# A three-stage chain (attention, gated feed-forward, mixture attention) on one core: a written table of the order of all operations, other PSUM banks, and filler products

## The chip, the cores and the metric

One Trainium2 chip, one of its cores. The time is microseconds (us) of device time of one execution. The kernel before was timed three times: 550.66, 550.70 and 551.35 us, median 550.7. Beside that one execution was profiled.

## The reference, cut to what matters

Four batches go through three stages, all in float32. Shapes: batch 4, 12 heads, 448 positions, head size 64, model size 768, inner size 1024, 4 experts.

```python
# 1: attention with a soft cap
scores = cap * tanh((q @ k.T) / 8 / cap)
attn = exp(scores - max) / (sum + 1e-9)
x = heads_side_by_side(attn @ v)              # [448, 768]
# 2: gated feed-forward with a convolution along the positions
h = maximum(x @ w_in, 0)                      # [448, 1024]
gate = 1 / (1 + exp(-conv3(h, conv_w)))
x = (h * gate) @ w_out                        # [448, 768]
# 3: four causal attention experts, the two best by x @ w_gate weighted
for e in range(4):
    y_e = softmax(causal((x @ wq[e]) @ (x @ wk[e]).T / 8)) @ (x @ wv[e]) @ wo[e]
out = sum(w_e * y_e)
```

## The kernel before, in words

Precision comes from splitting: a float32 value is written as a high part h that TensorE multiplies in its fast float32r form and a rest l, and a product is h·h + h·l + l·h, three TensorE products where one would do. Only the value products, the sums and the filler products run as plain float32; the profile counts each of these twice, since each is two passes.

Names of the stages, as used below. A *pair* is two heads that share 128 rows; a batch has six, numbered g = 0 to 23 over all batches. `qk` (line 560) makes the scores of a pair in four blocks of keys (three of 128, one of 64 that both heads share): products into PSUM, then ScalarE takes the hyperbolic tangent out of PSUM (896 columns for a block of two heads, 448 for the shared one) and the exponential (1792 and 1344 columns). `pv` (line 608) multiplies by the values. For g under `JOINT` it uses eight products per pair, each 128 rows by 64 columns of the array, and the shared block has rows of zeros for the other head. From `JOINT` on an even pair has six products and the odd one after it ten, of which four are 64 by 64, and two banks stay open, 7 and 2. `sums` and `recip` (lines 646, 662) give the sums of the exponentials and one over them, `x_unit` (line 744) spreads these over the head's rows by two products of 64 rows per unit, three units a batch: VectorE multiplies the attention output by them out of PSUM, ScalarE and VectorE split it into h and l. `f_unit` (line 755) multiplies by `w_in` in two half sums of nine products, `conv_gate` (line 778) makes convolution and gate in four ScalarE and four VectorE operations of 448 columns. For the first `EARLY_N[b]` of the eight row blocks of a batch that happens right behind `f_unit`; for the others `prep_g` (line 891) loads the raw h back from DRAM and does it later. `wi_prep` (line 730) decodes and splits `w_in` during batch 0: per piece one ScalarE absolute value of 256 columns and VectorE work. `fold_mm` folds `w_out` and the projection weights into one matrix between stage 2 and stage 3, after which per batch `v_unit`, `proj_unit`, `scores2`, `norm2`, `tr2`, `pv2` and `wo_unit` (lines 979 to 1163) do stage 3.

PSUM has eight banks of 512 columns. `qk` writes pairs of banks in turn, 3 and 4 and then 5 and 6. `pv` of batch 0 writes bank 1 for pairs 0, 2 and 4 and bank 7 for the others. `x_unit` takes banks 2, 0, 1 in a ring, `pv2` bank 7.

What sets the order. No engine's instructions are written in the order in which they run. Each call (`pl.mm`, `pl.act`, `pl.tt`, `pl.load` and so on) records an operation with its cost and the operations that it depends on (`Plan.add`, line 127). At the end `Plan.issue` (line 210) runs a list scheduler (`Plan.schedule`, line 154) several times, with costs, a wish for a place (`at`, shifted by the table `BIAS`) and windows, takes the order that ends first by its own reckoning, and issues every operation in that order. Each engine then works its own queue strictly in that order, and waits at an instruction until what that instruction needs is done. All DMAs stand in one queue, SP's.

So in the profile nearly all products have the line of a helper (305), all ScalarE operations 245, all VectorE operations 253, transposes 309, DMAs 314.

At the very start eight products of zeros (`WARM`) run on TensorE into bank 7 before the first data have landed.

Of the kernel before, what the change touches and what calls it, by code (L numbers as in the profile page):

```python
# [14 lines left out]
NP = H // 2  # L15
# [23 lines left out]
JOINT = 10  # L39
# [7 lines left out]
WARM = 8  # L47
ABS_DVE = (0, 0, 0, 0)
PV_1 = (0, 2, 4)
# [20 lines left out]
EARLY_N = (1, 7, 7, 0)  # L70
# [3 lines left out]
WINDOW = 0  # L74
STAY = 2000.0
ROUNDS = 5
# [14 lines left out]
class Plan:  # L91

    PAGE = 256


    DRAIN = 97.0
    OPEN = {(128, 128): 107.0, (64, 128): 107.0, (128, 64): 53.0, (64, 64): 53.0, (128, 32): 13.0}  # L100
    RATE = 320.0
    HOP = {"pe": 200.0, "act": 190.0, "dve": 170.0, "pool": 150.0, "dma": 1500.0}

    def __init__(self, nc):
        self.nc, self.ops, self.pos, self.seen, self.bias, self.kind = nc, [], 0.0, {}, 0.0, None

    def pages(self, ap):
# [19 lines left out]
    def add(self, eng, cost, calls, outs, ins, keys_out=(), keys_in=(), size=0, modes=None):  # L127
        op = Op()
        op.modes, op.kind = modes, self.kind
        op.eng, op.cost, op.calls, op.pos, op.n, op.size = eng, cost, calls, self.pos, len(self.ops), size  # L130
        op.after, op.bias = [], self.bias
        before = {}
        touched = [(k, w, False) for a in ins for k, w in self.pages(a)] + [(k, True, False) for k in keys_in]
        touched += [(k, w, True) for a in outs for k, w in self.pages(a)] + [(k, True, True) for k in keys_out]
        for key, whole, write in touched:
            past = self.seen.setdefault(key, [])
            for o, w in past:
                if (write or w) and o is not op:
                    before[o.n] = o
            if write and whole:  # L140
                past[:] = [(op, True)]
            elif (op, write) not in past:
                past.append((op, write))
        for o in before.values():
            o.after.append(op)
        self.ops.append(op)
        return op

    def latency(self, a, b):
        if a.eng == b.eng and a.eng != "dma":  # L150
            return 0.0 if a.eng == "pe" else 130.0
        return self.HOP[a.eng] + a.size / self.RATE

    def schedule(self, place, links, window, back=False):

        ops, todo = self.ops, [0] * len(self.ops)
        for l in links:
            for n, _ in l:
                todo[n] += 1
        ready, start, end = ([0.0] * len(ops) for _ in range(3))  # L160
        free, open_, pick, order = {}, {}, {}, []
        for e in self.HOP:
            free[e], open_[e] = 0.0, [o.n for o in ops if o.eng == e and not todo[o.n]]
        wire, cold, changed, mode, lands = 0.0, COLD_0, set(self.HOP), None, []
        if not back:
            free["dma"] = 800.0
        while len(order) < len(ops):
            for e in changed:
                if open_[e]:
                    t = max(free[e], min(ready[n] for n in open_[e])) + (window if e in ("pe", "act", "dve") else 0.0)  # L170
                    if e == "pe" and not back:
                        n = min((place[n] + (ops[n].modes[0] != mode) * STAY, n) for n in open_[e] if ready[n] <= t)[1]
                    else:
                        n = min((place[n], n) for n in open_[e] if ready[n] <= t)[1]
                    pick[e] = max(free[e], ready[n]), e, n
                    if e == "dma" and len(lands) >= 8:

                        pick[e] = max(pick[e][0], lands[-8]), e, n
                else:
                    pick.pop(e, None)  # L180
            t, e, n = min(pick.values())
            cost, more = ops[n].cost, 0.0
            if e == "pe" and not back:

                if t - free[e] > 2500.0:
                    cold = max(cold, t + 3600.0)
                if t < cold:
                    cost += min(cost, (cold - t) / 2)
                if ops[n].modes[0] != mode:
                    cost += self.DRAIN + self.OPEN[ops[n].modes[0]]  # L190
                mode = ops[n].modes[1]
# [1116 lines left out]
```

## Time and profile before

| | |
|---|---|
| median of three runs | 550.7 us |
| profiled execution, span of its instructions | 549.1 us |
| between the two (what lies around the span, and the spread of runs) | 1.6 us |
| TensorE products, busy | 539.9 us, 98% |
| VectorE, busy | 447.7 us, 82% |
| ScalarE, busy | 395.3 us, 72% |
| batch 0 of stage 1 | about 5 to 58 us |
| batches 1 to 3 of stage 1, with stage 2 of the batch before | to about 264 us |
| rest of stage 2, folding of the weights | to about 347 us |
| stage 3 of the four batches | to the end |

In the profile a product's end is modelled, so "busy" is no measure of how much faster TensorE could be; the distance from one start to the next is. "Idle before" names the engine that ended the wait. A row "x16" merges sixteen instructions of one form that follow each other.

### The profile page before, as it was taken

How to read it: one execution, taken by the hardware profiler on the slowest of the kernel's cores; microseconds unless marked ns; L12 is line 12 of the kernel's file. 1: busy time of each engine (PE TensorE's matmuls, PEld its weight loads, DVE VectorE, ACT ScalarE, POOL GpSimd, SP SyncE). 2: the span in 40 equal slices, each digit the busy share in tenths (PEclk: the TensorE clock that was granted, in tenths of full speed). 3: DMA queues.
4: the chain of work that ended last, by engine and by line, in shares of the span. 5: the costliest groups of instructions: out<-in, count | busy, mean ns of one | idle time of the engine just before them, and what ended most of it. 6: DMA issues, size and time to landing. Idle time of an engine off the chain costs nothing.

```text
span 549.1 us, 9130 instructions
## 1 busy us (share of the span) xinstructions
PE 539.9 (98%) x3170; PEld 420.1 (77%) x3170; DVE 447.7 (82%) x980; ACT 395.3 (72%) x736; POOL 24.5 (4%) x100
## 2 busy tenths in 40 slices
PE   7999999999999999999999999999999999999997
PEld 5444596556785567656799999989988997999886
DVE  6989999968788799878978999846867988946763
ACT  6999967898789997995645678625754977624751
POOL 8600000000000000000000000100000000000000
PEclk9999999999999999999999999999999999999999
DMA  7655425342224320224385632326433314413414
GB/s 257 194 184 171 152 91 162 110 124 87 65 86 122 109 84 32 77 83 121 111 240 164 219 115 73 108 70 149 112 91 104 97 53 123 126 45 87 105 57 145
DMA packets 38942, 64.61 MB, mean 118 GB/s; under 512 B 6896, under 2 KB 27632, under 8 KB 38896
## 3 DMA queue, kind: packets, MB, share of 16 engines
q1 hardware_dynamic: 38896, 64.02, 39.6%
q8 instruction: 25, 0.41, 0.3%
q14 instruction: 21, 0.17, 0.1%
HBM read 41.72 MB, written 12.85 MB: 99 GB/s over the span
## 4 chain that ended last, share of the span: by engine, by line
PE 78%; DVE 9%; ACT 8%; issue 2%; DMA 2%; SPq 0%; DVEq 0%; ACTq 0%
PE ps L305 76%; ACT fm L245 7%; DVE fm L253 6%; DVE rm L253 3%; PE ps L309 2%; ACT rm L245 1%; DMA fm<-w_in 1%; DMA fm<-g_dram 1%; SPq L314 0%; DVE ps L253 0%; DVEq L253 0%; ACTq L245 0%
## 5 line engine op out<-in xcount | busy, mean ns | idle before, releaser
L305 PE MATMUL ps<-rm 128*128 128x448 f32 (+4 forms) x2382 | 423.7, 355 | 4.8 <-ACT fm L245 3.7
L305 PEld LDWEIGHTS ps<-rm 128*128 128x128 f32 (+1 forms) x2382 | 367.8, 188 | 66.4 <-ACT fm L245 21.5
L245 ACT ACTIVATE fm<-fm 128x448 f32<-128x448 f32 (+8 forms) x247 | 178.0, 747 | 31.6 <-DVE fm L253 15.9
L253 DVE SCALAR_TENSOR_TENSOR fm<-fm 128x448 f32<-128x448 f32 (+5 forms) x281 | 164.1, 607 | 22.5 <-ACT fm L245 19.0
L245 ACT ACTIVATE fm<-ps,fm 128x896 f32<-128x896 f32 (+4 forms) x152 | 111.6, 760 | 30.7 <-DVE fm L253 24.2
L305 PE MATMUL ps<-fm 128*64 128x448 f32 (+6 forms) x660 | 111.0, 516 | 1.2 <-DVE fm L501 1.1
L253 DVE TENSOR_TENSOR rm<-fm,rm 128x448 fp32r<-128x448 f32 (+6 forms) x134 | 88.8, 683 | 5.1 <-ACT rm L245 4.6
L305 PEld LDWEIGHTS ps<-fm 128*64 128x64 f32 (+3 forms) x660 | 38.7, 136 | 57.8 <-issue 46.9
L245 ACT ACTIVATE fm<-ps 128x448 f32<-128x448 f32 (+3 forms) x131 | 53.5, 446 | 34.4 <-PE ps L305 27.0
L245 ACT ACTIVATE rm<-fm 128x448 fp32r<-128x448 f32 (+6 forms) x93 | 49.6, 562 | 23.3 <-DVE fm L253 15.3
L253 DVE TENSOR_TENSOR fm<-fm 64x448 f32<-64x448 f32 (+6 forms) x106 | 52.9, 512 | 4.5 <-ACT fm L245 2.3
L245 ACT ACTIVATE rm<-ps 128x386 fp32r<-128x386 f32 (+3 forms) x56 | 22.9, 424 | 29.7 <-PE ps L305 26.1
L253 DVE TENSOR_SCALAR fm<-fm 128x256 int32<-128x256 int32 (+8 forms) x101 | 29.7, 316 | 4.5 <-ACT fm L245 1.8
L253 DVE TENSOR_TENSOR ps<-ps,fm 128x128 f32<-128x128 f32 (+1 forms) x56 | 15.1, 286 | 17.2 <-PE ps L305 15.0
L253 DVE TENSOR_TENSOR rm<-ps,rm 128x386 fp32r<-128x386 f32 (+1 forms) x32 | 18.8, 589 | 11.6 <-ACT rm L245 11.5
L253 DVE CAST rm<-fm 128x960 fp32r<-128x960 f32 (+3 forms) x47 | 22.6, 484 | 6.8 <-PE ps L305 5.6
L253 DVE COPY fm<-ps 128x448 f32<-128x448 f32 (+2 forms) x37 | 20.4, 564 | 6.1 <-PE ps L305 5.4
L253 DVE TENSOR_REDUCE fm<-ps 128x1 f32<-128x128 f32 (+3 forms) x56 | 23.6, 446 | 0.4
L328 POOL MEMSET fm<- 64x1 f32 (+10 forms) x49 | 6.2, 143 | 356.9 <-PE ps L305 232.7
L253 DVE TENSOR_TENSOR fm<-fm,ps 128x448 f32<-128x448 f32 x30 | 17.6, 615 | 1.6 <-PE ps L305 1.4
L309 PE MATMUL ps<-fm 128*128 128x128 f32 x128 | 17.7, 275 | 0.2
L309 PEld LDWEIGHTS ps<-fm 128*128 128x128 f32 x128 | 14.6, 140 | 1.6 <-ACT fm L245 0.8
(19 smaller groups left out, 64.4 us busy)
## 6 DMA issues: line engine op xcount, KB each, us to landing
fm<-kq SPq DMA_DIRECT2D x23, 480.0 KB, 3.7
fm<-g_dram SPq DMA_DIRECT2D x33, 224.0 KB, 2.8
g_dram<-fm SPq DMA_DIRECT2D x32, 224.0 KB, 2.2
fm<-w_in SPq DMA_DIRECT2D x24, 256.0 KB, 3.8
fm<-woT SPq DMA_DIRECT2D x16, 384.0 KB, 3.3
out<-fm SPq DMA_DIRECT2D x23, 224.0 KB, 2.0
fm<-v SPq DMA_DIRECT2D x24, 192.0 KB, 2.5
rm<-rm SPq DMA_DIRECT2D x32, 128.0 KB, 2.3
```

The lines of the kernel that those rows point to most:

```text
L245: self.add("act", cost, [lambda: self.nc.scalar.activation(out, in_, func, **kw)], [out] + more, [in_] + ptr)
L253: self.add("dve", cost, [lambda: f(out, *ins, **kw)], [out], aps)
L305: self.nc.tensor.matmul(out, a, b, start=start, stop=stop, **kw))
L309: calls = [lambda o=o, i=i, d=d: self.nc.tensor.transpose(o, i, d) for o, i, d in parts]
L328: self.add("pool", cost, [lambda: f(out, *ins, **kw)], [out], [x for x in list(ins) + [kw.get("in_")] if hasattr(x, "ap")])
```

## The change

Every operation gets a fixed place: `ORDER` lists the numbers of all 2491 operations, and `issue` issues them so. `BIAS`, the scheduler and its constants go. Sixteen more filler products (`FILL`) are recorded, to be placed by the table like the rest, so 2475 operations become 2491. `Plan.add` now also makes any two operations of different engines that touch one PSUM bank keep the order in which they were recorded. The shared block of the value products is joined from pair 6 on instead of pair 10. The scores of batch 0 go over three pairs of banks (3 and 4, 5 and 6, 0 and 1) instead of two; its value products all use bank 7. The three `x_unit`s of batch 3 get a bank each instead of the ring of three. `pv2` of the second half uses bank 2. Of batches 1 and 2 four row blocks instead of seven get convolution and gate early. In `proj_unit` and `v_unit` the ScalarE operations on a bank are recorded ahead of the VectorE ones instead of in turn.

```diff
-JOINT = 10
+JOINT = 6
 WARM = 8
+FILL = 16
-PV_1 = (0, 2, 4)
+PV_1 = ()
-EARLY_N = (1, 7, 7, 0)
+EARLY_N = (1, 4, 4, 0)
...
+ORDER = tuple(map(int, '''
+0 45 71 1 56 90 66 25 81 2 58 113 50 1419 3 26 68 36 4 133 5 82 29 64 110 6 37 128 70 7 60 27 96 8 99 127 97 9 74 62
...
+'''.split()))
...
+        for b in {key[2] * self.PAGE // 2048 for key, _, _ in touched if key[0].startswith("ps")}:
+            users = self.banks.setdefault(b, [])
+            for o in users:
+                if o.eng != eng:
+                    before[o.n] = o
+            users.append(op)
...
     def issue(self):
...
+        for n in ORDER:
+            for call in self.ops[n].calls:
                 call()
...
+        at(-99, "warm")
+        for _ in range(FILL):
+            pl.mm([(bank(7)[:, :128], z, z, True, True)])
...
-        ps = banks[:, 3 + 2 * (c % 2):5 + 2 * (c % 2)]
+        f = ((3, 5, 0)[(4 * g + c) % 3] if g < NP else 3 + 2 * (c % 2))
+        ps = banks[:, f:f + 2]
...
-        ps = [XB.next()[:, :S] for _ in range(2)]
+        ps = [bank(k)[:, :S] for k in ((3, 4), (5, 6), (7, 2))[i]] if b == B - 1 else [XB.next()[:, :S] for _ in range(2)]
...
-            for a, t in ((slice(0, 128), slice(0, n)), (lo64, slice(n, n + 64)), (hi64, slice(n + 64, SG))):
-                s = slice(0, n) if t.start == 0 else slice(n, S)
+            for a, t, s in places:
                 pl.act(z[a, t], ps[a, s], AF.Copy, scale=D ** -0.5)
+            for a, t, s in places:
                 pl.stt(l[a, t], ps[a, s], D ** -0.5, f32(z[a, t]), OP.mult, OP.subtract)
...
-        ps = bank(7)
+        ps = R1 if i else bank(7)
...
-            wop.append(G2.next() if m < 2 else R1 if m == 2 else QB.next())
+            wop.append(G2.next() if m < 2 else bank(7) if m == 2 else QB.next())
```

What the table does to the order shows in the instructions of each engine. In the rows below a line is that of the helper, then come the operation, what it writes and reads (`ps` is PSUM, `fm` and `rm` are memory in float32 and in split form), its columns, and how many of them stand in a row.

First place, the start of TensorE's queue. `fm 128x128` are fillers, `rm 128x448` products of scores, `fm 64x448` value products (and the last part of the sums), `fm 32x448` sums. Before:

```order
L305 MATMUL ps<-fm 128x128 x8
L305 MATMUL ps<-rm 128x448 x39
L305 MATMUL ps<-fm 64x448 x8
L305 MATMUL ps<-rm 128x448 x9
L305 MATMUL ps<-fm 32x448 x4
```

Now, the same engine from its first instruction on:

```order
L340 MATMUL ps<-fm 128x128 x13
L340 MATMUL ps<-rm 128x448 x18
L340 MATMUL ps<-fm 128x128 x6
L340 MATMUL ps<-rm 128x448 x3
L340 MATMUL ps<-fm 128x128 x2
L340 MATMUL ps<-rm 128x448 x6
L340 MATMUL ps<-fm 128x128 x3
L340 MATMUL ps<-rm 128x448 x21
L340 MATMUL ps<-fm 64x448 x8
```

Thirteen fillers stand ahead of the first score product instead of eight, eleven more in three places between score products, and the first value product has 48 score products ahead of it instead of 39.

The same place on ScalarE, before. `ps,fm 128x896` and `ps,fm 128x448` are tangents, 1792 and 1344 columns exponentials, `fm<-fm 128x256` absolute values of `wi_prep`, `rm<-fm 128x256` its splitting copies:

```order
L245 ACTIVATE rm<-fm 128x128
L245 ACTIVATE fm<-fm 128x1
L245 ACTIVATE fm<-ps,fm 128x896 x2
L245 ACTIVATE fm<-fm 128x256
L245 ACTIVATE fm<-ps,fm 128x896
L245 ACTIVATE fm<-fm 128x1792
L245 ACTIVATE fm<-ps,fm 128x896
L245 ACTIVATE fm<-ps,fm 128x448
L245 ACTIVATE fm<-fm 128x256
L245 ACTIVATE fm<-fm 128x1344
```

ScalarE now:

```order
L280 ACTIVATE rm<-fm 128x128
L280 ACTIVATE fm<-fm 128x1
L280 ACTIVATE fm<-fm 128x256
L280 ACTIVATE fm<-ps,fm 128x896 x3
L280 ACTIVATE fm<-fm 128x1792
L280 ACTIVATE fm<-ps,fm 128x448
L280 ACTIVATE fm<-ps,fm 128x896
L280 ACTIVATE fm<-fm 128x1344
L280 ACTIVATE fm<-ps,fm 128x448
L280 ACTIVATE fm<-ps,fm 128x896 x2
```

The first absolute value moves ahead of the first tangent, the second behind the second pair's exponentials. Counted on to the last exponential of batch 0, ScalarE's queue has 63 operations before and 57 now: three absolute values, one splitting copy, one copy of a value product out of PSUM and one of 24 columns have moved behind it. The tangents and exponentials ahead are the same.

Second place, TensorE in batch 1, from its first value products on. Before, with four pairs of eight products (the rows of 8), then six and ten:

```order
L305 MATMUL ps<-fm 64x448 x8
L305 MATMUL ps<-rm 128x448 x143
L305 MATMUL ps<-fm 64x448 x8
L305 MATMUL ps<-fm 32x448 x4
L305 MATMUL ps<-rm 128x448 x18
L305 MATMUL ps<-fm 64x448 x8
L305 MATMUL ps<-rm 128x448 x12
L305 MATMUL ps<-fm 64x448 x8
```

Now, from the same pair on:

```order
L340 MATMUL ps<-fm 64x448 x6
L340 MATMUL ps<-rm 128x448 x41
L340 MATMUL ps<-fm 64x448 x10
L340 MATMUL ps<-rm 128x448 x102
L340 MATMUL ps<-fm 64x448 x6
L340 MATMUL ps<-fm 32x448 x4
L340 MATMUL ps<-rm 128x448 x39
L340 MATMUL ps<-fm 64x448 x10
```

Eight and eight have become six and ten. Over the whole queue, the form of the array's tiles (rows by columns) changes 139 times from one product to the next before and 131 times now, though the two more joined pairs add two such changes inside a pair.

Third place, VectorE where stage 1 ends. RECIPROCAL, CAST and the `rm<-rm,fm` operation are `recip` of batch 3; `fm<-fm,ps` are the multiplications of `x_unit` out of PSUM, `rm<-fm,rm 128x448` its splitting, 772 columns the splitting of projection weights, `fm<-fm` SCALAR_TENSOR_TENSOR are of `conv_gate`. Before:

```order
L253 RECIPROCAL fm<-fm 128x448
L253 SCALAR_TENSOR_TENSOR fm<-fm 128x448
L253 CAST rm<-fm 128x448
L253 TENSOR_TENSOR rm<-fm,rm 128x772
L253 SCALAR_TENSOR_TENSOR rm<-rm,fm 128x448
L253 SCALAR_TENSOR_TENSOR fm<-fm 128x448 x3
L253 TENSOR_TENSOR fm<-fm,ps 128x448 x3
L253 TENSOR_TENSOR rm<-fm,rm 128x448 x3
L253 TENSOR_TENSOR fm<-fm,ps 128x448 x3
L253 TENSOR_TENSOR rm<-fm,rm 128x448 x3
```

Now:

```order
L288 RECIPROCAL fm<-fm 128x448
L288 CAST rm<-fm 128x448
L288 SCALAR_TENSOR_TENSOR fm<-fm 128x448
L288 SCALAR_TENSOR_TENSOR rm<-rm,fm 128x448
L288 SCALAR_TENSOR_TENSOR fm<-fm 128x448
L288 TENSOR_TENSOR rm<-fm,rm 128x772
L288 TENSOR_TENSOR fm<-fm,ps 128x448 x3
L288 SCALAR_TENSOR_TENSOR fm<-fm 128x448
L288 TENSOR_TENSOR fm<-fm,ps 128x448 x2
L288 TENSOR_TENSOR rm<-fm,rm 128x772
L288 TENSOR_TENSOR rm<-fm,rm 128x448 x2
```

The work is the same. On TensorE, three half sums of nine `f_unit` products of batch 2 now stand between the sums that `recip` reads and the six products of `x_unit`, and four more such half sums between these and the first `f_unit` of batch 3. Before, four half sums stood between the sums and the `x_unit`s, and the first `f_unit` of batch 3 followed directly behind these.

## Rows read from the trace of the kernel before

**Rows 1.** The page's first lines: span, busy time of TensorE and its share.

```profile
span 549.1 us, 9130 instructions
...
PE 539.9 (98%) x3170; PEld 420.1 (77%) x3170; DVE 447.7 (82%) x980; ACT 395.3 (72%) x736; POOL 24.5 (4%) x100
```

**Rows 2.** The page's chain that ended last, shares of the span by line.

```profile
PE ps L305 76%; ACT fm L245 7%; DVE fm L253 6%; DVE rm L253 3%; PE ps L309 2%; ACT rm L245 1%; DMA fm<-w_in 1%; DMA fm<-g_dram 1%; SPq L314 0%; DVE ps L253 0%; DVEq L253 0%; ACTq L245 0%
```

**Rows 3.** Stretches: length, busy PE, PEld, DVE, ACT, POOL; TensorE's granted clock; DMA.

```profile
6.00:12.40 6.40, 3.58 (x25) 1.96 (x23) 5.23 (x14) 6.01 (x7) 5.62 (x39) 1.00 0.94 315
12.40:15.90 3.50, 3.50 (x16) 2.08 (x18) 3.50 (x6) 3.11 (x5) 3.31 (x11) 0.51 0.47 175
15.90:50.00 34.10, 33.48 (x205) 14.88 (x201) 31.44 (x75) 33.48 (x47) 7.30 (x17) 1.00 0.64 197
```

**Rows 4.** TensorE's start in order of time: start, duration, work, idle before.

```profile
1.11 3.78 PE L305 MATMUL ps<-fm 128*128 128x128 f32 x16 [1.11 <-DVE fm L501]
4.83 1.97 PE L305 MATMUL ps<-rm 64*128 64x448 f32 x12
...
12.25 2.48 PE L305 MATMUL ps<-rm 64*128 64x448 f32 x12 [1.70 <-ACT fm L245]
```

**Rows 5.** ScalarE's first tangents, in order of time.

```profile
6.17 1.91 ACT L245 ACTIVATE fm<-ps,fm 128x896 f32<-128x896 f32 x2 [0.54 <-PE ps L305]
8.29 0.44 ACT L245 ACTIVATE fm<-fm 128x256 f32<-128x256 f32 x1 [0.22 <-DMA fm<-w_in]
```

**Rows 6.** ScalarE's forms: count, busy us, mean ns, idle before.

```profile
L245 ACT ACTIVATE fm<-ps 128x448 f32<-128x448 f32 x82 | 44.2, 544 | 20.6 <-PE ps L305 14.0 <-PE ps L309 5.1 <-DMA fm<-woT 1.0
...
L245 ACT ACTIVATE fm<-fm 128x256 f32<-128x256 f32 x30 | 13.2, 449 | 5.2 <-DMA fm<-w_in 3.7 <-DVE fm L253 1.0 <-DMA fm<-kq 0.4
```

**Rows 7.** TensorE's value products of batch 1, in order of time.

```profile
99.17 3.23 PE L305 MATMUL ps<-fm 128*64 128x448 f32 x16
...
112.64 2.48 PE L305 MATMUL ps<-fm 128*64 128x448 f32 x12
115.05 4.92 PE L305 MATMUL ps<-rm 64*128 64x448 f32 x30
119.90 3.39 PE L305 MATMUL ps<-fm 128*64 128x448 f32 x20
```

**Rows 8.** The end of stage 1, in order of time.

```profile
257.59 2.94 DVE L253 RECIPROCAL fm<-fm 128x448 f32<-128x448 f32 x1
259.70 4.70 PE L305 MATMUL ps<-rm 128*128 128x448 f32 x22
...
263.92 0.19 PEld L305 LDWEIGHTS ps<-rm 64*128 64x128 f32 x2 [0.31 <-issue]
...
264.43 1.69 DVE L253 TENSOR_TENSOR fm<-fm,ps 128x448 f32<-128x448 f32 x3
...
268.84 3.52 PE L305 MATMUL ps<-rm 128*128 128x448 f32 x16 [0.15 <-DVE fm L253]
```

**Rows 9.** A projection's bank emptied in stage 3, in order of time.

```profile
362.62 0.59 ACT L245 ACTIVATE rm<-ps 128x384 fp32r<-128x384 f32 x2 [3.59 <-PE ps L305]
...
363.25 0.56 DVE L253 SCALAR_TENSOR_TENSOR rm<-ps,rm 128x384 fp32r<-128x384 f32 x1 [3.75 <-ACT rm L245]
...
364.62 2.70 PE L305 MATMUL ps<-rm 128*128 128x448 f32 x12 [0.59 <-DVE rm L253]
```

**Rows 10.** Waits of TensorE for ScalarE, whole span: total, times, longest.

```profile
PE ps L305 <- ACT fm L245: 3.7, 6, 1.7
```

**Rows 11.** Busy time by stretch in stage 3, columns as in Rows 3.

```profile
365.00:380.00 15.00, 15.00 (x78) 13.91 (x76) 7.71 (x35) 4.80 (x14) 0.00 (x0) 1.00 0.50 115
380.00:395.00 15.00, 14.83 (x105) 14.03 (x104) 13.99 (x39) 10.65 (x32) 0.11 (x1) 1.00 0.60 153
```

**Rows 12.** Forms that `conv_gate` is made of, VectorE's and ScalarE's.

```profile
L253 DVE SCALAR_TENSOR_TENSOR fm<-fm 128x448 f32<-128x448 f32 x128 | 81.9, 650 | 14.9 <-ACT fm L245 14.2
...
L245 ACT ACTIVATE fm<-fm 128x448 f32<-128x448 f32 x128 | 75.1, 598 | 13.6 <-DVE fm L253 9.2 <-DVE rm L253 1.7 <-DMA fm<-g_dram 1.2
```

More of the change, by code (lines that the diff above doesn't have):

```diff
@@ L78 @@
-WINDOWS = (0.0, 50.0, 200.0)
-COLD_0 = 5500.0
+ORDER = tuple(map(int, '''
[99 rows of a table added]
+'''.split()))
 T_ORDER = ("q0", "q1", "tr0", "tr1", "pv0", "tr2", "tr3", "pv1", "wo")
@@ L105, in __init__ @@
         self.nc, self.ops, self.pos, self.seen, self.bias, self.kind = nc, [], 0.0, {}, 0.0, None
+        self.banks = {}
     def pages(self, ap):
@@ L152, in latency @@
         return self.HOP[a.eng] + a.size / self.RATE
[L154 to L191, printed above, removed]
-            start[n], end[n], free[e] = t, t + cost, t + cost
-            if e == "dma" and not back:
-                wire = max(wire, end[n] + 500.0) + ops[n].size / self.RATE
-                late = 1400.0 if 1000.0 < t < 12000.0 else 600.0
-                lands.append(max(wire + 1000.0 + late, end[n] + self.HOP["dma"] + ops[n].size / self.RATE))
-                more = lands[-1] - end[n] - self.HOP["dma"] - ops[n].size / self.RATE
-            order.append(n)
-            open_[e].remove(n)
-            changed = {e}
-            for m, l in links[n]:
-                todo[m] -= 1
-                ready[m] = max(ready[m], end[n] + l + more)
-                if not todo[m]:
-                    open_[ops[m].eng].append(m)
-                    changed.add(ops[m].eng)
-        return start, end, order
@@ L210, in issue @@
-    def issue(self):
-        ops = self.ops
-        after = [[(o.n, self.latency(op, o)) for o in op.after] for op in ops]
-        before = [[] for _ in ops]
-        for op in ops:
-            for n, l in after[op.n]:
-                before[n].append((op.n, l))
-        done = lambda s: max(s[1][o.n] + (o.eng == "dma") * 2000.0 for o in ops)
-        last = best = self.schedule([o.pos for o in ops], after, WINDOW)
-        for _ in range(ROUNDS):
-            _, ends, _ = self.schedule([-x for x in last[1]], before, WINDOW, back=True)
-            place = [o.bias - ends[o.n] for o in ops]
-            last = min((self.schedule(place, after, w) for w in WINDOWS), key=done)
-            best = min(best, last, key=done)
-        for n in best[2]:
-            for call in ops[n].calls:
+    def issue(self):
+        assert sorted(ORDER) == list(range(len(self.ops)))
+        place = {n: i for i, n in enumerate(ORDER)}
+        assert all(place[op.n] < place[o.n] for op in self.ops for o in op.after)
+        for n in ORDER:
+            for call in self.ops[n].calls:
@@ L398, in at @@
     def at(pos, kind=None):
-        pl.pos, pl.bias, pl.kind = pos, BIAS.get(kind, 0.0), kind
+        pl.pos, pl.bias, pl.kind = pos, 0.0, kind
     def f32(x):
@@ L503, in chain_kernel @@
             pl.mm([(bank(7)[:, :128], z, z, True, True)])
+        at(-99, "warm")
+        for _ in range(FILL):
+            pl.mm([(bank(7)[:, :128], z, z, True, True)])
+    at(-100, "st")
     load(0)
@@ L1031, in v_unit @@
         else:
-            for x, a in ((V2[b][:, t], lo64), (VS, hi64)):
+            both = (V2[b][:, t], lo64), (VS, hi64)
+            for x, a in both:
                 pl.act(x[64:], ps[a, :NV], AF.Copy)
+            for x, a in both:
                 pl.copy(x[:64, E * D:], ps[a, E * D:NV])
```

6 lines of the change are left out of this document (2 added, 4 removed), and 98 rows, old and new, of the table ORDER.

## The prediction, made before the changed kernel was run

> **What bounds the kernel now.** I read the page's head first, then the chain, then the stretches, then the places where TensorE waited. TensorE is busy 539.9 of 549.1 us [rows 1], and 78% of the chain that ended last are its products [rows 2]. So for most of the span a change is worth what it takes from TensorE's own queue, and what another engine saves is worth nothing. The stretches show the exceptions. From 6.0 to 50.0 us ScalarE is busy 6.01 + 3.11 + 33.48 = 42.6 of 44.0 us [rows 3]: there the tangents and exponentials of batch 0 set the pace. [...] The other exception is the end of stage 1 near 264 us, where TensorE waits for VectorE [rows 8], and short waits for emptied banks in stage 3 [rows 9]. The span is 549.1 us, the median of the runs 550.7, so 1.6 us lie around the span; I make the sum on the span and add 1.6.
>
> **Batch 0.** Up to the last exponential of batch 0 ScalarE loses six operations from its queue: three absolute values at 0.449, one splitting copy of 256 columns, which I take at the same 0.449, one copy out of PSUM at 0.544 [rows 6], and one of 24 columns, which I take at half of the first. That is 1.35 + 0.45 + 0.54 + 0.22 = 2.56 us. Against it stand the fillers. Before, eight take 3.78 us, 0.47 each, and the first score product starts at 4.83 [rows 4], the first tangent 1.34 us later, at 6.17 [rows 5]. Five more fillers stand ahead of it now. At 0.47 each the first score product would start at 1.11 + 13 × 0.47 = 7.2; if each takes half as long from the ninth on, at 1.11 + 3.78 + 1.18 = 6.1. That delays the first tangent by 1.2 to 2.4 us less what the operands cost anyway; a score product of the first three groups also waits less for its parts, which are all there by then, so I take 0.9. The absolute value that waited for its DMA to 8.29 [rows 5] and held back the third tangent now stands in the idle time ahead of the first tangent: its 0.44 and its 0.22 of waiting are gained, if its DMA, which is now issued ahead of the second pair's load, lands by then; I count 0.3. The third pair of banks takes away tangents' waits for products, 0.2 at most. The eleven later fillers stand between score products that feed ScalarE; while it is the bound they are hidden, and if that cover goes they cost 11 × 0.24 to 11 × 0.47, 2.6 to 5.2 us. Some of them aren't covered: I charge 1.0. Sum: −2.56 + 0.9 − 0.3 − 0.2 + 1.0 = −1.2 us. Bounds: −2.7 (no delay by fillers after the start) and +2.5.
>
> The low clock is no term of its own. [...]
>
> **Value products.** Pairs 6 to 9 go from eight and eight to six and ten. Eight show as 16 records and 3.23 us, six as 12 and 2.48, ten as 20 and 3.39 [rows 7]. Per two pairs 6.46 − 5.87 = 0.59, twice 1.18. These stand where TensorE is the bound: −1.2 us. Their price can't be off by more than 0.2. The joined pair holds bank 2, which the sums use too; that wait is in the last term.
>
> **Changes of the tiles' form.** 139 become 131, and two of these are inside the joined pairs and paid above, so ten fewer. Four records more cost 3.23 − 2.48 = 0.75, so the 12 are worth 2.25, but the next form starts 2.41 after the first [rows 7]: 0.16 for a change at each end, 0.08 each. Ten: −0.8 us, between 0 and −1.0.
>
> **End of stage 1.** From 263.92, the weights of the first `x_unit`, to 268.84, the second `f_unit` half of batch 3, pass 4.92 us [rows 8]. In it TensorE does six short products in pairs, 0.3 a pair at most, and nine of the kind of which 22 take 4.70, 1.92. So 4.92 − 0.9 − 1.92 = 2.1 us are waiting for VectorE and for banks. Now four half sums, 4 × 1.92 = 7.7 us, stand behind the `x_unit`s. VectorE needs until then five multiplications and some splits at 1.69/3 = 0.56, one of 772 columns three times at 0.95 (the rows around show no other size; 772/448 × 0.56) and two of `conv_gate`: 11 × 0.56 + 3 × 0.95 + 0.65 = 9.6 at most, of which the last are needed only by the later products; I keep 0.3 of waiting. Ahead, three half sums, 5.8 us, cover a gather, which I take at 0.56 like the multiplications, the reciprocal's 2.94 and three operations at up to 0.65 [rows 12], together 5.5: just covered, 0.2 kept. −2.1 + 0.5 = −1.6 us, between 0 and −2.1.
>
> **Stage 3, the emptied bank.** A projection is copied out by ScalarE and VectorE in turn from 362.62 on; TensorE's next projection into that bank starts at 364.62 after an idle 0.59 [rows 9]. Now two half projections into the other bank, 2 × 2.4, stand between. −0.6, between 0 and −0.7. [...]
>
> **Hidden edits.** Fewer early gates move 6 × (4 × 0.650 + 4 × 0.598) [rows 12] = 15.6 us of VectorE and 14.4 of ScalarE from stage 1 into stage 3, at nothing while TensorE has work. `pv2` in bank 2 and the last stores: 0, between −0.5 and +0.3.
>
> **New waits.** A table that orders 2491 operations has waits of its own. All of TensorE's waits for ScalarE before are 3.7 us [rows 10]; those outside the start sum to well under 1. A new order may have as many, or save as many: from −1.5 to +4, I take +0.4.
>
> **Sum.** −1.2 − 1.2 − 0.8 − 1.6 − 0.6 + 0.4 = −5.0. 549.1 − 5.0 = 544.1 on the span, 545.7 as a run.
>
> **Rivals.** First, most of the gain is given back in batch 0: all its value products use bank 7, so each waits until ScalarE has copied the last one out, and the copy stands in the queue of the engine that is the bound. For: ScalarE's 42.6 of 44.0 [rows 3]. Against: three groups of scores or more stand between two value products. Price: five waits of a copy (0.54) and a half of a tangent's pair (1.91/4), 5 × 1.0, so −5.0 + 5.0, or 550.7: no change.
>
> Second, slower: VectorE becomes the bound in stage 3. It has 13.99 of 15.00 us filled from 380 to 395, though only 7.71 in the 15 before [rows 11]. Three units of batch 2's gates, 3 × 2.6 = 7.8 us, come into these 30, which makes 29.5 of 30. The gates of batch 1 stand similarly ahead of their projection. A unit alone is a chain of 4 × 0.650 + 4 × 0.598 = 5.0 us; if the last one is late by its length and a split of 1.2, the projections wait 6.2, for both batches 12.4: 545.7 + 6.2 to 12.4 = 552 to 558. It decides from 6.1 us of such waiting on. Against: in the order most gates stand some three half projections ahead of their use.
>
> Third, fully covered: the small scattered waits go too. Then batch 0 gives its −2.7, the end of stage 1 −2.1, new waits −1.5: −2.7 − 1.2 − 1.0 − 2.1 − 0.7 − 1.5 = −9.2, or 541.5. For: TensorE's queue has work of another bank between users of one bank in each place I looked at. Against: the fillers' cost at the start.
>
> **How the numbers follow.** Forecast as above (543 to 548.5) 0.60, fully covered 0.20, gain given back 0.13, slower 0.07. A measurement tells 0.2%, about 1.1 us, from no change: faster means under 549.6. Of the case "given back" a third falls there, half within, the rest above. Faster 0.60 + 0.20 + 0.04 = 0.84, same 0.07, slower 0.09. Range for 8 in 10: 541.5 to 549.8.
>
> **What would show it.** Right: the last exponential of batch 0 ends 1 to 2 us earlier; granted clock at full from 6 to 50 us; the value products of batch 1 in 12 and 20 records; no idle above 0.5 us of TensorE between `x_unit`s and the first `f_unit` of batch 3, and that stretch 3 to 5 us earlier; in stage 3 no idle of 0.59 at the second projection. Wrong: a first tangent after 8 us; a chain that goes through VectorE between 350 and 450 us; a low clock in the start; or TensorE's total idle time at or above the 9.2 us (549.1 − 539.9) of before.

## The result, and the profile after

The changed kernel takes 545.43 us (median of four runs, 544.65 to 546.63) against 550.98 for the kernel before (four runs, 550.66 to 551.35): ratio 0.990, 95% interval 0.9883 to 0.9918. Faster by 5.5 us, where 5.0 was forecast (545.7). The sum that gave this was not right in all its terms: batch 0 gave less than forecast, the end of stage 1 and the term for new waits gave more, and these errors partly cancelled.

The page of the profiled execution, one of the shorter two of the four, first its head, then the chain:

```profile
span 543.0 us, 9129 instructions
...
PE 535.7 (99%) x3202; PEld 421.2 (78%) x3202; DVE 445.9 (82%) x980; ACT 389.2 (72%) x736; POOL 22.1 (4%) x100
...
PE ps L340 81%; ACT fm L280 5%; DVE fm L288 3%; PE ps L344 3%; POOL fm L363 3%; DVE rm L288 2%; ACT rm L280 1%; POOL rm L363 0%; POOLq L363 0%; POOL fm masks.py:199 0%; POOL fm masks.py:197 0%; POOLq masks.py:199 0%; DVEq L288 0%; ACTq L280 0%; POOLq L1344 0%
```

Against [rows 1, 2] the span is 6.1 us shorter and TensorE's idle time 543.0 − 535.7 = 7.3 us in place of 9.2. VectorE's share of the chain fell from 9% to 5%, but GpSimd has come in with 3%, where it had no share worth a place before.

The same stretches as in [rows 3], and two of stage 3 as in [rows 11] (length, busy PE, PEld, DVE, ACT, POOL, granted clock, DMA):

```profile
6.00:12.40 6.40, 6.33 (x50) 5.17 (x49) 3.51 (x6) 5.94 (x7) 5.75 (x31) 1.00 0.76 263
12.40:15.90 3.50, 3.26 (x26) 2.34 (x26) 2.99 (x5) 3.50 (x5) 3.24 (x13) 1.00 0.77 198
15.90:50.00 34.10, 31.93 (x196) 14.26 (x196) 30.57 (x69) 32.24 (x43) 4.99 (x18) 1.00 0.54 171
...
365.00:380.00 15.00, 15.00 (x96) 14.21 (x95) 12.44 (x32) 8.70 (x24) 0.00 (x0) 1.00 0.70 191
380.00:395.00 15.00, 15.00 (x95) 14.24 (x94) 14.21 (x50) 10.63 (x32) 0.00 (x0) 1.00 0.29 79
```

The granted clock is full in these stretches. But ScalarE, which had 33.48 of 34.10 us filled from 15.9 to 50.0, has 32.24 now: the engine that sets the pace stands still for 1.9 us. Its timeline shows where; the last row is the last exponential of batch 0:

```profile
6.45 0.43 ACT L280 ACTIVATE fm<-fm 128x256 f32<-128x256 f32 x1 [1.44 <-DMA fm<-w_in]
6.89 2.81 ACT L280 ACTIVATE fm<-ps,fm 128x896 f32<-128x896 f32 x3
...
16.43 3.09 ACT L280 ACTIVATE fm<-fm 128x1792 f32<-128x1792 f32 x2
21.37 0.46 ACT L280 ACTIVATE fm<-fm 128x256 f32<-128x256 f32 x1 [1.86 <-POOL rm L363]
...
22.17 0.42 ACT L280 ACTIVATE fm<-fm 128x256 f32<-128x256 f32 x1
22.49 0.99 ACT L280 ACTIVATE fm<-ps,fm 128x896 f32<-128x896 f32 x1
...
51.29 1.42 ACT L280 ACTIVATE fm<-fm 128x1344 f32<-128x1344 f32 x1
```

In the kernel before, that exponential (1.42 us, in a row with a short operation behind it) starts later:

```profile
52.10 1.76 ACT L245 ACTIVATE fm<-fm 128x1344 f32<-128x1344 f32 x2
```

GpSimd's cast of the selector of the sums (the constant with which `x_unit` spreads the sums over the heads' rows; 24 selects write it), before and then now:

```profile
7.54 1.24 POOL L328 CAST rm<-fm 128x768 fp32r<-128x768 f32 x1
```

```profile
19.93 1.41 POOL L363 CAST rm<-fm 128x768 fp32r<-128x768 f32 x1
```

TensorE's timeline at the start, behind that wait, at the first joined pair, and at the two places further on:

```profile
1.11 4.94 PE L340 MATMUL ps<-fm 128*128 128x128 f32 x26 [1.11 <-DVE fm L536]
5.99 2.08 PE L340 MATMUL ps<-rm 64*128 64x448 f32 x18
8.00 1.60 PE L340 MATMUL ps<-fm 128*128 128x128 f32 x12
...
24.73 1.68 PE L340 MATMUL ps<-rm 128*128 128x448 f32 x9 [1.42 <-ACT fm L280]
...
61.13 2.48 PE L340 MATMUL ps<-fm 128*64 128x448 f32 x12
70.45 3.39 PE L340 MATMUL ps<-fm 128*64 128x448 f32 x20
...
250.67 34.61 PE L340 MATMUL ps<-rm 128*128 128x448 f32 x171
...
349.77 22.46 PE L340 MATMUL ps<-rm 128*128 128x260 f32 x123
```

The absolute value at 21.37 writes over the memory from which GpSimd casts the selector of the sums. In the kernel before, 31 of GpSimd's instructions stood ahead of this cast, and it ended at 8.78; the table has put 86 ahead of it, and it ends at 21.34. ScalarE waits for it, TensorE behind ScalarE. The last two rows are without an "idle before" for 34.6 and 22.5 us: the end of stage 1 and the projections of stage 3, where [rows 8] and [rows 9] had waits.

TensorE's waits over the span, whole (compare [rows 10]):

```profile
PE ps L340 <- ACT fm L280: 2.4, 4, 1.4
PE ps L340 <- DVE fm L536: 1.1, 1, 1.1
```

Where the time came from can be laid out by stretch. For every operation on TensorE (one recorded call, which can hold many products) I took the distance to the next start, less the usual distance for its kind (the lower quartile in the kernel before; fillers count as loss whole). Lost so, in us, with what the prediction's terms foresaw in the last column:

| stretch (us) | before | after | difference | foreseen |
|---|---|---|---|---|
| 0 to 60, batch 0 | 11.7 | 11.2 | −0.5 | −1.2 |
| 60 to 250 | 2.1 | 1.5 | −0.6 | in +0.4 |
| 250 to 280, end of stage 1 | 2.6 | 0.0 | −2.6 | −1.6 |
| 280 to 400 | 2.5 | 1.6 | −0.9 | −0.6 |
| 400 to the end | 3.8 | 4.1 | +0.4 | in +0.4 |
| the products themselves | 521.4 | 519.2 | −2.2 | −1.2 − 0.8 |

The differences are taken before rounding; together −6.4, and 0.3 comes back behind the last product, which leaves the 6.1 us of the spans. How it is parted depends on what counts as one kind. By an operation's own form alone the products themselves give −1.2 and batch 0 −0.9; if the form of what follows is taken in, −2.4 and −0.3. The −2.6 at the end of stage 1 and the −0.9 behind it stand either way.

### The profile page after: what moved, and what is told of

Same layout as the page of the kernel before. It is cut to its first block, busy times and chain, and to the rows that moved or that the text cites. A ratio compares the mean times of both kernels' runs of the same rounds, so it can differ in the third digit from the quotient of the medians.

```text
span 543.0 us, 9129 instructions
## 1 busy us (share of the span) xinstructions
PE 535.7 (99%) x3202; PEld 421.2 (78%) x3202; DVE 445.9 (82%) x980; ACT 389.2 (72%) x736; POOL 22.1 (4%) x100
## 4 chain that ended last, share of the span: by engine, by line
PE 84%; ACT 6%; DVE 4%; POOL 3%; issue 2%; POOLq 0%; DVEq 0%; ACTq 0%
PE ps L340 81%; ACT fm L280 5%; DVE fm L288 3%; PE ps L344 3%; POOL fm L363 3%; DVE rm L288 2%; ACT rm L280 1%; POOL rm L363 0%; POOLq L363 0%; POOL fm masks.py:199 0%; POOL fm masks.py:197 0%; POOLq masks.py:199 0%; DVEq L288 0%; ACTq L280 0%; POOLq L1344 0%
## 5 line engine op out<-in xcount | busy, mean ns | idle before, releaser
L340 PE MATMUL ps<-rm 128*128 128x448 f32 (+5 forms) x2382 | 419.1, 353 | 2.8 <-ACT fm L280 2.4
L280 ACT ACTIVATE fm<-fm 128x448 f32<-128x448 f32 (+7 forms) x247 | 177.6, 748 | 30.3 <-DVE fm L288 21.8
L280 ACT ACTIVATE fm<-ps,fm 128x896 f32<-128x896 f32 (+4 forms) x152 | 113.3, 765 | 41.7 <-DVE fm L288 31.1
L288 DVE TENSOR_TENSOR rm<-fm,rm 128x448 fp32r<-128x448 f32 (+4 forms) x134 | 88.3, 677 | 6.4 <-ACT rm L280 5.8
L340 PEld LDWEIGHTS ps<-fm 128*64 128x64 f32 (+3 forms) x692 | 41.8, 138 | 57.2 <-issue 48.6
L280 ACT ACTIVATE rm<-fm 128x448 fp32r<-128x448 f32 (+7 forms) x93 | 49.7, 563 | 17.5 <-DVE fm L288 11.7
L288 DVE TENSOR_SCALAR fm<-fm 128x256 int32<-128x256 int32 (+7 forms) x101 | 30.5, 317 | 4.8 <-DMA fm<-w_in 2.5
L288 DVE TENSOR_REDUCE fm<-ps 128x1 f32<-128x256 f32 (+3 forms) x56 | 24.5, 446 | 0.3
```

The costliest lines, as they stand in the source:

```text
L280: self.add("act", cost, [lambda: self.nc.scalar.activation(out, in_, func, **kw)], [out] + more, [in_] + ptr)
L288: self.add("dve", cost, [lambda: f(out, *ins, **kw)], [out], aps)
L340: self.nc.tensor.matmul(out, a, b, start=start, stop=stop, **kw))
```

## The experiments

All times are medians with the ratio to the kernel before, run on the same chip. The changed kernel is at 0.990 (0.9883 to 0.9918). The kernel before was timed again beside each series of runs; its four medians go from 550.98 to 551.71 us, so between runs of different series some 0.7 us say nothing.

**GpSimd's cast first.** The selects and the cast of the selector move to the head of GpSimd's queue, other engines' queues are unchanged (from the order of GpSimd's instructions):

```diff
+L363 AFFINE_SELECT fm<-fm 128x64 x24
+L363 CAST rm<-fm 128x768
+L363 MEMSET fm 128x96
...
-L363 MEMSET fm 64x1
-L363 ISA
-L363 AFFINE_SELECT fm<-fm 128x64
...
```

> The changed kernel with GpSimd's queue in another order: the operations that make the selector of the sums (24 selects and the cast to split form) come first, the ones and zeros that the sums need second, the rest last. Nothing else moves. In the changed kernel ScalarE stands idle for 1.86 us, from 19.51 to 21.37, until that cast ends, because the second absolute value of w_in overwrites the cast's source; TensorE waits 1.42 us for ScalarE right behind it, at 24.73. Theory A (ScalarE's queue sets the end of batch 0, so its wait passes on whole): the idle 1.86 is gone, TensorE's wait at 24.7 is under 0.3, the last exponential of batch 0 ends at 51.2 plus or minus 0.4 in place of 52.71, and the time is 1.2 to 1.9 us under the changed kernel's 545.4: 543.5 to 544.2. Rival B (TensorE is as full by then, the wait is taken up elsewhere): the wait goes, but the time falls by less than 0.5 us.

Measured: 543.58 us, 0.9862 (0.9848 to 0.9875), 1.85 less than the changed kernel, and the intervals don't touch. ScalarE in this kernel, and GpSimd's cast:

```profile
16.29 3.41 ACT L280 ACTIVATE fm<-fm 128x1792 f32<-128x1792 f32 x3
19.60 0.53 ACT L280 ACTIVATE fm<-ps 128x448 f32<-128x448 f32 x1
...
49.14 1.42 ACT L280 ACTIVATE fm<-fm 128x1344 f32<-128x1344 f32 x1
```

```profile
10.17 0.82 POOL L363 CAST rm<-fm 128x768 fp32r<-128x768 f32 x1
```

No wait of ScalarE is left there, and the last exponential ends at 50.56, not 52.71 (A had 51.2, give or take 0.4). Theory A holds against B: the time fell by far more than 0.5 us, and by what A gave. How much of the 1.85 is the wait itself is less sure. All four runs here have a mean clock of 1.000, the changed kernel only in two of its four; these two took 544.7, and against them the gain is 1.2. No trace shows where the clock fell in the other two. This kernel beats both.

**Without the sixteen fillers.**

```diff
         for n in ORDER:
+            if self.ops[n].kind == "warm":
+                continue
```

> The changed kernel without its sixteen new fillers (their products are not issued; the eight of before remain); all else in the table's order. The fillers take 4.2 us of TensorE's first 13. Theory A (they cost little and bring little: the first tangent waits for operands and for its absolute value, the later ones stand where ScalarE is behind anyway): the granted clock falls for some us before 20 us as it did in the kernel before, the first tangent comes at 6.4 to 6.9 us, and the time is within 0.7 us of the changed kernel's 545.4. Rival B (the gain of the change is the clock that they hold up): slower by 1.7 us or more, 547.1 and above. Rival C (a filler delays what stands behind it by its whole length): faster by 1.5 us or more, under 544.

Measured: 545.27, 0.9896 (0.9882 to 0.9911): no change, as A has it. But the profiled execution had the clock full (mean 0.999, 545.34 us) and the first tangent at 6.36; ScalarE then waited 2.73 us for the cast in place of 1.86:

```profile
21.90 0.44 ACT L282 ACTIVATE fm<-fm 128x256 f32<-128x256 f32 x1 [2.73 <-POOL rm L365]
```

The other three runs had mean clocks of 0.994 to 0.997 and took 545.19 to 545.86, about the same. With the cast late, what happens ahead of 21 us hardly counts. So the same was tried with the cast early:

> The run with GpSimd's queue put right, and in addition without the sixteen new fillers. In the run without fillers alone, the first tangent came at 6.36 in place of 6.89 us and ScalarE lost that again in a longer wait for GpSimd's cast (TensorE waited 2.7 us behind it), the granted clock stayed full all the same. Theory A (fillers delay batch 0 by what they delay the first tangent, and only the cast hid that): faster than the 543.6 of that run by 0.3 to 0.9 us, about 543.0. Rival B (the fillers are hidden anyway): within 0.3 of 543.6. Rival C (with the cast early TensorE idles more in the first 16 us and the clock falls): slower by 0.7 us or more.

Measured: 545.81, 0.9897 (0.9882 to 0.9912): 2.2 us slower than with the fillers (1.9 by the two ratios), rival C. From 6.0 to 18.5 us, first with, then without fillers:

```profile
6.00:12.00 6.00, 6.00 (x49) 5.11 (x49) 3.15 (x6) 5.64 (x7) 5.50 (x21) 1.00 0.88 295
12.00:18.50 6.50, 5.97 (x39) 3.22 (x38) 5.52 (x11) 6.50 (x7) 5.58 (x44) 1.00 0.68 219
```

```profile
6.00:12.00 6.00, 2.89 (x21) 1.68 (x17) 2.43 (x4) 5.10 (x6) 5.21 (x37) 0.99 0.78 249
12.00:18.50 6.50, 5.40 (x24) 3.63 (x21) 5.55 (x10) 4.94 (x6) 5.80 (x28) 0.50 0.77 241
```

And TensorE's 21 score products of that stretch, in the same order:

```profile
12.76 2.91 PE L340 MATMUL ps<-rm 128*128 128x448 f32 x21 [0.53 <-ACT fm L280]
```

```profile
13.44 5.14 PE L342 MATMUL ps<-rm 128*128 128x448 f32 x21 [1.10 <-ACT fm L282]
```

Without fillers TensorE was busy 2.89 of the six microseconds ahead, then the clock was granted at half (0.50 from 12.0 to 18.5) and the score products took 5.14 us, where they take 2.91 with fillers. ScalarE, 6.50 of 6.50 there, has 4.94 here: the slow products are not hidden. All five runs have mean clocks of 0.993 or 0.994. The idle time ahead is not all due to the missing fillers: in this execution the next pair's load landed later, and VectorE, whose splitting TensorE waits for, stood idle 2.98 us for it, against 0.97 with fillers. But in the run with eleven fillers, below, it was 2.49, and the clock held.

**Which fillers.** The early cast, without the five ahead of the first score product, and without the eleven behind it:

```diff
         for n in ORDER:
+            if 9 <= n <= 13:        # the other run: 14 <= n <= 24
+                continue
```

> The run with GpSimd's queue put right, without the first five of the sixteen new fillers (those ahead of the first score product); the eleven later ones remain. Without all sixteen the granted clock was 0.50 from 12 to 18 us, 21 score products took 5.14 us in place of 2.9, and the time was 545.8 in place of 543.6. Theory A (the eleven fill the gaps in which TensorE had waited before the clock fell; the five only delay the first tangent by 0.4 us): clock full, 543.0 to 543.4. Rival B (five and eleven are both hidden): 543.6 plus or minus 0.3. Rival C (the clock falls without the five too): 545 or more.

> The counterpart: the five fillers ahead of the first score product remain, the eleven later ones are left out. Theory A (the later ones hold the clock): granted clock near 0.50 for several us between 12 and 19, 545.2 to 546.2. Rival B (any fillers do): clock full, 543.6 plus or minus 0.4.

Measured: with the eleven alone 543.20, 0.9839 (0.9817 to 0.9861); with the five alone 545.89, 0.9888 (0.9871 to 0.9906). The intervals don't touch: the eleven hold the clock, the five don't. From 12.0 to 18.5, the eleven, then the five:

```profile
12.00:18.50 6.50, 6.26 (x45) 3.76 (x43) 4.39 (x8) 6.20 (x6) 5.69 (x31) 1.00 0.80 219
```

```profile
12.00:18.50 6.50, 5.40 (x25) 3.85 (x23) 5.38 (x10) 4.48 (x5) 5.83 (x30) 0.50 0.78 242
```

Whether dropping the five gains anything isn't settled: the first tangent comes earlier (6.46, not 6.79), but 543.20 and 543.58 are from different series, their intervals overlap, and the last exponential of the profiled run was not earlier (it ended at 51.15, not 50.56).

And none of the 24 fillers, the eight old ones left out too:

> As before, but with none of the 24 fillers, so that TensorE does nothing until the first operands of the scores are there. The eight old fillers take 3.78 us and end at 4.89, the first score product follows at once at 4.83. Theory A (the operands are there at about 4.8, the eight fillers only lift the clock): the first score products run at half the granted clock or a little above, the first tangent is 0.3 to 0.7 us later than without the sixteen, and the time is 0.5 to 2 us above that run. Rival B (ScalarE is the bound and hides slow score products): within 0.4 us of the run without the sixteen. Rival C (the eight fillers held the first score product back): faster by more than 0.4.

```diff
         for n in ORDER:
+            if 1 <= n <= 24:
+                continue
```

Measured: 545.61, 0.9898 (0.9883 to 0.9914), the same as without the sixteen. That is rival B's number, but not its reason: the granted clock is at 0.50 in both for some microseconds between 12 and 20 us (from 12 to 18 without the sixteen, from 14 to 16 without any), the 21 score products take 5.14 and 4.43 us, where they take 2.91 with fillers, and ScalarE doesn't hide it. The eight old fillers alone bring nothing that shows.

**The end of stage 1 put back**, with the old ring of banks and with the new banks. The first two lines are the order on TensorE (1054, 1061 and 1068 are the `x_unit`s of batch 3); ScalarE's and VectorE's operations on them move along:

```diff
-938 942 1068 1061 1054 939 943 946 947 1165
+938 942 939 943 946 947 1054 1061 1068 1165
...
-ps = [bank(k)[:, :S] for k in ((3, 4), (5, 6), (7, 2))[i]] if b == B - 1 else [XB.next()[:, :S] for _ in range(2)]
+ps = [XB.next()[:, :S] for _ in range(2)]          # ring run only
```

> The changed kernel with the end of stage 1 put back: the three x_units of batch 3 use the old ring of banks 2, 0 and 1, and so stand behind the four half sums of batch 2's f_unit instead of ahead of them; ScalarE's and VectorE's operations on them follow in the same order. All else as in the table. Theory A (the stretch is worth what the waits in it say): TensorE waits for VectorE in three or four places between the x_units and the second f_unit of batch 3, together 2 to 2.7 us, and the time is 1.8 to 2.7 us above the changed kernel's 545.4: 547.2 to 548.1. Rival B (what is late there is made up by slack before the folding of weights): within 0.6 of 545.4.

> As the run with the x_units of batch 3 behind the four half sums on the ring, in the same order of all operations, but with the six new banks, one per unit and half. It parts the banks from the order. Theory A (the order does it: the four half sums cover VectorE's multiplications and splits; without them the first f_unit of batch 3 waits for these, whatever the banks): TensorE no longer waits between the x_units, 1.3 us less there, but waits longer at the f_units behind, and the time is 1.2 to 2.5 us above the changed kernel's 545.4. Rival B (the banks do it): the time is within 0.5 us of 545.4, though the order is that of before.

Measured: with the ring 553.15, 1.0034 (1.0019 to 1.0049), 7.7 us above the changed kernel; with the new banks 550.91, 0.9998 (0.9984 to 1.0013), 5.5 above. Both are far over what A gave. TensorE with the new banks, and the stretches around, in the longest of its twelve runs (553.53), in which the clock fell from 27.7 to 31.0 us as well:

```profile
267.47 2.95 PE L340 MATMUL ps<-rm 128*128 128x448 f32 x7 [2.74 <-DVE fm L288]
```

```profile
264.00:268.00 4.00, 1.26 (x8) 0.85 (x9) 3.52 (x7) 2.39 (x5) 0.00 (x0) 0.83 0.51 183
268.00:274.00 6.00, 6.00 (x19) 5.35 (x18) 5.35 (x10) 2.90 (x6) 0.00 (x0) 0.55 0.18 12
274.00:280.00 6.00, 6.00 (x31) 5.46 (x30) 3.60 (x9) 2.01 (x5) 0.00 (x0) 1.00 0.60 203
```

The wait is near the size expected, 2.74 us in one piece, but then the clock falls: 19 products in six microseconds, where the next six hold 31. Of its runs the one with a mean clock of 1.000 took 548.52, 3.8 above the changed kernel's two such runs (544.7). So by this one run the order alone is worth 3 to 4 us, and some 2.4, from 548.52 to the median, go with the clock. With the ring TensorE waits longer for ScalarE, and the 0.51 for VectorE comes on top:

```profile
265.31 0.68 PE L340 MATMUL ps<-rm 64*128 64x448 f32 x3 [3.05 <-ACT fm L280]
266.50 4.02 PE L340 MATMUL ps<-rm 64*128 64x448 f32 x9 [0.51 <-DVE fm L288]
```

The order counts for more than the banks (5.5 against a further 2.2, both with what the clock adds), as A said. The kernel before had this order and ring and lost only 2.6 us, its waits being short ones: putting the order back inside the table is dearer than it was in the place it came from.

**The emptied bank of stage 3 put back.**

```diff
-1480 1503 1504 1520
+1480 1520 1503 1504
```

> The changed kernel with one place of stage 3 put back: the first half of the second projection, which goes into the bank that the first projection has just left, follows directly, ahead of the two half projections into the other bank; ScalarE's three and VectorE's three parts of the emptying are moved up with it. In the kernel before, the emptying took from 362.58 to 364.57, 2.0 us, of which a half sum of 1.6 covered all but 0.59. Theory A (the wait comes back, and here whole): TensorE waits 1.7 to 2.1 us there for VectorE and the time is 1.5 to 2.1 above the changed kernel's 545.4: 546.9 to 547.5. Rival B (TensorE catches it up by slack behind): within 0.5 us. Rival C (the wait makes the granted clock fall): above by 3 us or more.

Measured: 550.00 (547.59 to 551.01), 0.9964 (0.9946 to 0.9983), 4.6 above the changed kernel's 545.43, or 3.5 by the two ratios.

```profile
361.73 4.66 PE L340 MATMUL ps<-rm 128*128 128x448 f32 x14 [2.00 <-DVE rm L288]
```

```profile
362.00:366.50 4.50, 4.50 (x16) 4.03 (x16) 4.50 (x12) 2.29 (x5) 0.00 (x0) 0.62 0.72 190
366.50:372.00 5.50, 5.50 (x29) 5.08 (x28) 0.17 (x2) 1.22 (x4) 0.00 (x0) 1.00 0.01 3
```

The wait is 2.00 us, as A worked out from [rows 9]; then the clock falls again, rival C. The one run of nine with a mean clock of 1.000 took 547.59, 2.9 above the changed kernel's 544.7 at that clock: the wait, and 0.9 that no row here explains.

**One part alone, under the old planner.**

```diff
-JOINT = 10
+JOINT = 6
```

> The kernel before, with its planner, with one part of the change: the value products joined from pair 6 on in place of pair 10. The planner makes its order anew. Theory A (the products are worth what they take on TensorE): 2 x 0.59 us less, 549.6 to 550.2 against 551.1. Rival B (the planner's new order decides, by waits elsewhere): more than 1 us from that on either side.

> The kernel before, with its planner, with one part of the change: a bank each for the six halves of batch 3's x_units. Theory A (banks alone take the waits between the x_units away, 0.70 and 0.63 us, and the planner leaves the four half sums ahead of them): 1.3 us less, 549.5 to 550.1 against 551.1. Rival B (the f_units of batch 3 then wait as much longer for VectorE's splits): within 0.5 us of 551.1. Rival C (freed of the ring, the planner moves the x_units ahead by itself): 2 us less or better.

The second run has the new banks alone (the line shown above, in the kernel before). Measured: 556.58, 1.0097 (1.0075 to 1.0120), and 555.49, 1.0076 (1.0058 to 1.0095). Rival B in the first case; in the second none of the three: slower by 4.5. In the first, the planner's new order loses 7.5 us between 60 and 250, where the old one lost 2.1, by waits such as

```profile
65.60 1.55 PE L305 MATMUL ps<-rm 64*128 64x448 f32 x3
68.09 2.09 PE L305 MATMUL ps<-rm 64*128 64x448 f32 x11 [0.94 <-DVE fm L253]
```

and has the clock at 0.57 from 272 to 276. In the second, the new order loses some 2 us more than the old one between 60 and 250 and as much again between 250 and 280, where the clock is at 0.50 from 270 to 273. Under the old planner, then, neither edit gains anything by itself; the new order that the planner makes costs more. The joined pairs under the table were not tried alone, since the table fits one list of operations and another `JOINT` makes another list. Their worth stands on the rows alone, and so does that of the three pairs of banks in batch 0, of the fewer early gates, and of bank 2 for `pv2`.

## Why the prediction was right or wrong

**Batch 0: right in sign, too large, and wrong in three of its terms.** The sum was −1.2; TensorE gained 0.5 (0.3 to 0.9 by the reckoning above), and the last exponential ended 0.8 earlier, less than the 1 to 2 announced. That ScalarE sets the pace there holds. TensorE had the same 33.48 of 34.10 us busy, but a product's recorded time is longer than its distance to the next (0.365 us and 0.20 for one of 128 rows and 448 columns), and by the distances TensorE lost 11.7 us in batch 0. From the first tangent to the last exponential of batch 0 pass 47.35 us before (ScalarE busy 46.12, idle 1.23), 45.82 now (43.93 and 1.89), and 43.77 with the cast early (43.73 and 0.04).

The delay by fillers was sized well: the last five fillers took half of the first eight's time each (1.16 / 5 = 0.23 us against 3.78 / 8 = 0.47), the first score product started at 5.99 (6.1 worked out), the first tangent at 6.89 (7.07).

The first step that failed is the one that counted what ScalarE's queue loses and looked at its waits for TensorE and DMA, not for GpSimd, whose queue the change had also reordered. That wait is 1.86 us long, and the run with the cast early gained 1.85 (1.2 between runs of full clock).

The second is the size of the two terms on ScalarE. The six operations that have left its queue, and the absolute value that has moved ahead of the first tangent, were priced at 2.56 + 0.44 = 3.0; ScalarE's busy time between these two fell by 46.12 − 43.93 = 2.2. They were priced by their mean length, but in the record an operation starts before the one ahead of it has ended: one of 256 columns at 22.17 lasts 0.42, and the next starts at 22.49, 0.32 behind it. Against that the old waits, 1.23 in all, are all gone, where at most 0.2 + 0.22 were counted.

The third is "the low clock is no term of its own". My ground was [rows 3], where ScalarE was busy 3.11 of 3.50 us in the stretch with the clock at 0.51. With the cast early the four corners are

| | cast late | cast early |
|---|---|---|
| sixteen fillers | 545.43 | 543.58 |
| none of them | 545.27 | 545.81 |

The fillers are worth 2.2 us (1.9 by the ratios) and the early cast 1.85, but each only with the other. My reading is that a late cast hides slow products (without fillers the runs of lower clock took no longer than the one of full clock), and slow products hide an early cast; in single operations this was not followed. With the cast early the slow products' price shows in the row itself: 5.14 − 2.91 = 2.2 us for 21 of them. The charge of 1.0 for the later eleven fillers did not come: with the cast late, leaving all sixteen out gained nothing, and with it early the eleven brought 545.89 − 543.58 = 2.3 (1.4 by the ratios).

**Value products: right; tile forms: not parted.** Six and ten show as 12 records in 2.48 us and 20 in 3.39, as in [rows 7]. Products and form changes together gave −2.2 for the −2.0 foreseen, and the products by their own form alone −1.2, just their term. That the rest is the changes of form rests on how the kinds are counted.

**End of stage 1: right place, too small.** −1.6 foreseen, −2.6 measured. The 0.3 and the 0.2 us that I kept as waiting did not come: no row there has an idle time. And the wait before was larger than 2.1: in the changed kernel the six short products take 0.81 and a half sum 1.83, not 0.9 and 1.92, which leaves 4.92 − 0.81 − 1.83 = 2.3. The last 0.3 lies elsewhere in the thirty microseconds. The first `f_unit` of batch 3 starts at 261.8, not 266.6 as before, as announced (3 to 5 us earlier).

**Emptied bank: right.** No idle time at the second projection; −0.6 foreseen, −0.9 for the whole stretch from 280 to 400.

**Hidden edits and new waits: right.** No wait of TensorE for VectorE is left but the one at the start. New waits took +0.4 in the sum; the stretches from 60 to 250 and from 400 on lost 0.2 less, so this term had the wrong sign.

**The rivals.** "Given back by bank 7" did not occur: the second pair's value products of batch 0 started at 26.34, their bank empty since 22.26, and all four waits of TensorE for ScalarE sum to 2.4. "VectorE becomes the bound" neither: it was busy 12.44 + 14.21 = 26.7 of 30 us, not 29.5, and its share of the chain fell. "Fully covered" (541.5) did not come either; with the early cast the kernel is half way to it, at 543.6, though by other terms.

**The total.** That 5.5 came where 5.0 was forecast is in part luck. On the spans, batch 0 gave 0.7 less than its term; the end of stage 1 gave 1.0 more, new waits 0.6, the stretch from 280 to 400 0.3 and the products 0.2, and 0.3 came back behind the last product: 6.1 in the executions that were profiled.

What the prediction left out altogether is the second price of a wait. Both places put back cost more than their wait, and in the profiled executions the clock fell behind it: the median lies 2.4 us above the one run with a full clock in both (550.91 − 548.52, 550.00 − 547.59). Two of the changed kernel's own four runs have a mean clock of 0.997 and take 546.15 and 546.63, the other two 1.000 and 544.7; in all four runs with the early cast it is 1.000.

## What to carry to other kernels

When a change reorders queues, go through every engine's queue for what each operation on the bounding engine waits for, GpSimd's setup work too: an operation that is off the path can be put behind 55 more and come onto it. Price an operation in a full queue by the distance to the next start, not by its own length (0.32 us against 0.42 for the one at 22.17). Price a new wait of TensorE twice, once by its length and once by the clock behind it (2.4 us more at the median in each of the two places put back), and test two suspected causes together as well as one by one, since each can hide the other. Where the clock differs from run to run, set runs of full clock against runs of full clock. A part of a change that was planned together may be worth nothing, or less, alone.

## What the runs showed of the hardware

Fillers did not have to be many. With GpSimd's cast early, eleven, placed where TensorE would have waited between 8 and 13 us, held the mean granted clock at 0.999 or 1.000 in all four runs; eight or thirteen ahead of the first product did so in none of eleven. After single waits of 2.0 and 2.7 us of a TensorE that was otherwise full the clock fell to 0.50 for some three to seven microseconds in the profiled executions, though one of nine runs and one of twelve kept a mean clock of 1.000; after the short waits of [rows 8], 2.6 us in sum, it had not fallen. Nor did it fall after a wait of 2.68 us at 22.6 in the run without fillers and with the cast late, so the length of a wait alone did not decide it.

GpSimd's cast of 768 columns took 1.41 us beside a VectorE at work on two-input operations (1.24 in the kernel before, beside one of these and a cast), and 0.82 in the run with the early cast, where VectorE stood idle from 10.01 to 11.82 us. The rows give no reason for the difference, and no run was made to find one; they show when the operations ended. Where GpSimd's cast started behind a VectorE operation, it ended 0.68 us behind that operation's end (20.66 and 21.34 in the changed kernel, 8.09 and 8.77 in the kernel before). Where it started first, the end of a VectorE cast of 960 columns, 0.66 us long otherwise, came 0.63 us behind its own (9.71 and 10.34 with the eleven fillers, 9.81 and 10.44 with the five).
